# Second batch's attention heads as row-tiled pairs, with pair-wide values buffers and three rotating score buffers

## The chip, the cores and the metric

The kernel runs on one core of a Trainium2 chip. The time is the device time of one execution in microseconds, and the figure compared is the median of several runs. TensorE is called PE below, VectorE DVE, ScalarE ACT, GpSimd POOL, and SP is the engine whose queue issues nearly all DMA transfers of this kernel.

## The reference

Three stages follow one another: an attention over 4 batches of 8 heads (576 positions, head size 64), a gated MLP on its output, and a mixture of 8 experts with a route that is sticky along the sequence. Only the attention matters for the change:

```python
scores = scale * np.matmul(q, k.transpose(0, 1, 3, 2))
cum = np.cumsum(np.maximum(s, 0.0), axis=-1)
bias = -(cum[:, :, :, None] - cum[:, :, None, :])
scores = np.where(causal, -1000000000.0, scores + np.minimum(bias, 0.0))
attn = softmax(scores)          # maximum taken off, sum + 1e-09
out = np.matmul(attn, v)
```

## The kernel before, in words

**Precision.** float32 products are made of split operands: a value x is kept as a rounded part "hi" and the rest "lo", and a product takes hi·hi + hi·lo + lo·hi. The bias of a head is the cumulated sum `cum`, kept as 10 rows (5 query tiles, hi and lo) that a matmul with a 0/1 selection adds to the scores.

**Tiles.** A head has five query tiles `i`: four of 128 queries with 128·(i+1) keys, and a last one of 64 queries, which the two heads of a pair share as one 128-row tile (`emit_tail`, with block-diagonal queries `bdq` and selection `bdr` or `bds`). `prep_T` (L365) transposes q and k of a pair into a tile of four planes (q hi, k hi, q lo, k lo), head 0 of the pair on partitions 0 to 63, head 1 on 64 to 127.

**Two ways to the scores.** The first batch (pairs 0 to 3, `p < PR`) uses `emit_R` (L482): the two heads of a pair go through PE with 64 contraction rows each, one in the upper and one in the lower half of the array, four matmuls for each head and query tile (three of split products, one for the bias, from the constant `selc` and the bias rows `cumr`). The other three batches use `emit_S` (L501), one head at a time: `prep_asm` (L389) builds a stacked copy of the head by five DMAs (three from the pair's planes, 885 kB together: (3 + 1 + 2) planes of 64 x 576 floats; one of the head's 10 bias rows; the first time for each buffer also the selection rows `sel`), so that two matmuls of 128 and 74 contraction rows are enough for a query tile. `QK[0]` and `QK[1]` hold the stacked copies (in the first batch the pairs' planes), `QK[2]` the planes of the later pairs.

**Softmax and values.** `row_min` (L437, DVE) takes the scores out of PSUM with mask and row extreme, `soft` (L444) makes exp on ACT, adds 1e-9 on POOL, takes the reciprocal on DVE and scales on POOL. `emit_T` (L519) transposes the scaled tile on PE and copies it from PSUM into `et` by ACT or DVE. `emit_PV` (L544) multiplies by the values; heads 0 to 7 (`g < F4`) do it in plain float32. `emit_X` (L587) hands a pair's output on. In `emit_R` the first head's scaled tiles for i = 2, 3 lie in `E2`, `E3` (one buffer each), the second head's in tiles of the tag `ga` (two buffers for i = 2 and 3 together), which the MLP uses later.

**Order.** `R_steps` (L616) goes through the pairs of the first batch, five steps each; the list `AFTER` (L712) says how many steps later a pair's transposes (T), value products (P), value loads (V) and output (X) come, and what is over at the end (`left`) is worked off among the first steps of `A_steps` (L656), which handles the other heads with a lag of four tiles. `merge` interleaves a batch's attention with the MLP of the batch before (`M_steps`, L882; with `M0_steps`, L1443, for batch 0, which also prepares w_sg and w_out), by running sums of written costs; the MLP of batch 0 begins when the output of pair 3 is out. During the first batch the weights w_in are split (`W_steps`, L1418). A scheduler sets each engine's final order from this order by a simulated timeline. All loads and copies go through SP's queue in order (`dma`, L77). `prep_V` (L410) loads the values of one head into one of two buffers `vv`.

## Time and profile before

| what | value |
|---|---|
| median of 3 runs | 829.77 us (826.39 to 830.7) |
| the profiled execution's own time | 832.37 us |
| its span | 830.1 us |
| busy, share of span: PE | 785.8 us, 95% |
| PE weight loads | 675.5 us, 81% |
| DVE | 510.2 us, 61% |
| ACT | 436.0 us, 53% |
| POOL | 337.4 us, 41% |
| attention of batch 0 alone | from 10 us to about 80 us of the span |
| attention of batch 1 beside the MLP of batch 0 | about 80 us to 190 us |
| experts | from about 540 us |

The span is what the profile covers; the execution's own time adds what lies around it (2.3 us here). A busy PE means that at least one matmul is in the array by a modelled end, so it also counts the time in which a matmul only drains. The granted clock of PE is given as a share of full speed.

### The profile page before, as it was taken

The numbers are of one execution on the slowest core, as the hardware profiler recorded it, in microseconds if no ns is written. First come the engines' busy times: TensorE is split into PE (matmuls) and PEld (weight loads), VectorE is DVE, ScalarE is ACT, GpSimd is POOL, SyncE is SP. The second block draws the span as 40 slices with busy tenths as digits, with TensorE's granted clock in tenths as the row PEclk, the third lists the DMA queues.
The fourth block names the chain that finished last, engine by engine and source line by source line (L and its number), as shares of the span: only waits on it lengthen the run. The fifth ranks groups of instructions, "written<-read, shape, count | busy, mean of one in ns | idle before, by whom it ended". The sixth has DMA issues, their size and how long they took to land. (4 is left out here: it accounts for less than half of the span.)

```text
span 830.1 us, 14670 instructions
## 1 busy us (share of the span) xinstructions
PE 785.8 (95%) x4832; PEld 675.5 (81%) x4832; DVE 510.2 (61%) x1469; ACT 436.0 (53%) x1040; POOL 337.4 (41%) x614
## 2 busy tenths in 40 slices
PE   9887989899999999999999999989999999999995
PEld 5565877698789799789797778778988989899894
DVE  6787567685776789676884577664644445443420
ACT  6776567675547786246873254144544444444410
POOL 6787436575625578325684010060031220313101
PEclk9999999999999999989999999999999999999998
DMA  8568599845787575768442842153664444635401
GB/s 189 140 188 229 145 267 263 216 145 119 159 254 200 121 219 128 193 199 197 97 155 79 279 143 109 58 191 128 164 212 144 137 165 129 200 113 174 128 4 36
DMA packets 118041, 133.06 MB, mean 160 GB/s; under 512 B 69603, under 2 KB 83043, under 8 KB 117963
## 3 DMA queue, kind: packets, MB, share of 16 engines
q1 hardware_dynamic: 114123, 122.61, 53.6%
q0 software_dynamic: 3840, 9.48, 3.2%
q8 instruction: 40, 0.66, 0.3%
q14 instruction: 38, 0.31, 0.1%
HBM read 90.99 MB, written 22.95 MB: 137 GB/s over the span
## 5 line engine op out<-in xcount | busy, mean ns | idle before, releaser
L1241 DVE TENSOR_TENSOR wp<-wraw,wp 128x1024 fp32r<-128x1024 f32 x63 | 76.6, 1224 | 95.8 <-ACT wp L1240 91.3
L871 PE MATMUL ps<-wp,hT 128*128 128x512 f32 x528 | 123.0, 392 | 0.0
L871 PE MATMUL ps<-xT,wp 128*128 128x384 f32 x672 | 119.1, 336 | 0.0
L871 PEld LDWEIGHTS ps<-xT,wp 128*128 128x128 f32 x672 | 117.3, 188 | 0.7
L871 PEld LDWEIGHTS ps<-wp,hT 128*128 128x128 f32 x528 | 98.6, 188 | 21.1
L1297 POOL DMA_INDIRECT out_dram<-y,ids x24 | 29.4, 1224 | 212.3 <-ACT y L1296 175.0
L1240 ACT CAST wp<-wraw 128x1024 fp32r<-128x1024 f32 x64 | 66.5, 1049 | 62.6 <-DMA wraw<-in_moe_w_dram 56.0
L446 ACT ACTIVATE E<-E,negm 128x128 f32<-128x128 f32 (+4 forms) x136 | 79.4, 585 | 34.3 <-DVE negm L439 30.6
L450 POOL TENSOR_SCALAR E<-E,lsum 128x128 f32<-128x128 f32 (+4 forms) x136 | 77.8, 575 | 37.1 <-DVE lsum L448 28.3
L570 PE MATMUL ps<-et,vv 128*128 128x320 f32 (+9 forms) x476 | 82.5, 314 | 8.5 <-DVE et L537 5.2
L570 PEld LDWEIGHTS ps<-et,vv 128*128 128x128 f32 (+1 forms) x476 | 65.7, 173 | 22.8 <-DVE et L537 6.2
L439 DVE CUSTOM_DVE_ANT_0 E<-ps,zmask 128x128 f32<-128x128 f32 (+4 forms) x136 | 63.5, 471 | 17.9 <-PE ps L871 14.6
L447 POOL TENSOR_SCALAR lsum<-lsum 128x1 f32<-128x1 f32 (+1 forms) x128 | 31.2, 244 | 104.6 <-ACT E L446 88.3
L531 PE MATMUL ps<-ident,E 128*128 128x128 f32 (+1 forms) x452 | 67.6, 262 | 4.6 <-POOL E L450 1.6
L539 ACT CAST et<-ps 128x384 fp32r<-128x384 f32 (+3 forms) x120 | 50.2, 427 | 37.2 <-PE ps L531 35.3
L871 PE MATMUL ps<-wsg,vg 128*128 128x288 f32 x448 | 67.7, 302 | 0.8 <-DVE g L880 0.8
L871 PE MATMUL ps<-xh,w 128*128 128x288 f32 x256 | 59.3, 309 | 4.6 <-DVE wsg L857 2.9
L871 PEld LDWEIGHTS ps<-wsg,vg 128*128 128x128 f32 x448 | 62.0, 191 | 1.4 <-DVE g L880 1.0
L531 PEld LDWEIGHTS ps<-ident,E 128*128 128x128 f32 (+1 forms) x452 | 47.4, 140 | 16.5 <-issue 4.6
L540 DVE TENSOR_TENSOR et<-ps,et 128x384 fp32r<-128x384 f32 (+3 forms) x120 | 57.0, 481 | 4.6 <-ACT et L539 4.1
L871 PE MATMUL ps<-w,vg 128*128 128x512 f32 (+1 forms) x216 | 55.4, 400 | 0.0
L1285 DVE SCALAR_TENSOR_TENSOR hT<-ps,hT 128x384 fp32r<-128x384 f32 x56 | 30.3, 554 | 40.2 <-ACT hT L1284 40.0
(312 smaller groups left out, 1569.9 us busy)
## 6 DMA issues: line engine op xcount, KB each, us to landing
wraw<-in_moe_w_dram SPq DMA_DIRECT2D x64, 512.0 KB
qk<-qk SPq DMA_DIRECT2D x24, 432.0 KB
w<-wv_d SPq DMA_DIRECT2D x16, 512.0 KB
w<-wo_d SPq DMA_DIRECT2D x16, 512.0 KB
qk<-qk SPq DMA_DIRECT2D x24, 288.0 KB
w<-wu_d SPq DMA_DIRECT2D x12, 512.0 KB
nq<-in_q_dram SPq DMA_DIRECT2D x30, 144.0 KB
nk<-in_k_dram SPq DMA_DIRECT2D x30, 144.0 KB
```

The costliest lines, as they stand in the source:

```text
L439: hred[g] = DVE.tensor_tensor_reduce(out=e[:, a:z], in0=pt[:, 0:z - a], in1=zmask[:, m0:m0 + z - a], scale=-1.0, scalar=BIG if hi == 0 els ...
L446: ACT.activation(out=x, in_=x, func=ACTF.Exp, scale=-1.0, bias=nm, accum_out=l[:, z:z + 1])
L447: POOL.tensor_scalar(out=l, in0=l, scalar1=1e-9, scalar2=0.0, op0=ALU.add, op1=ALU.add)
L450: POOL.tensor_scalar(out=x, in0=x, scalar1=l[:, z:z + 1], scalar2=1.0, op0=ALU.mult, op1=ALU.mult)
L531: PE.transpose(pt[:, j * M:(j + 1) * M], e[h, 128 * j:128 * (j + 1)], ident[h, h])
L539: ACT.copy(out=dst[0], in_=src)
L540: DVE.tensor_tensor(out=dst[1], in0=src, in1=f32v(dst[0]), op=ALU.subtract)
L570: PE.matmul(x, lhsT=l, rhs=rhs if g >= F4 else f32v(rhs), start=(j == 0 and n_ == 0), stop=(j == js[-1] and n_ == len(ms) - 1),)
L871: ms = [PE.matmul(pt, lhsT=l, rhs=r, start=(first_ and x == 0), stop=(last_ and x == n - 1)) for x, (l, r) in enumerate(pairs)]
L1240: c = ACT.copy(out=w[:, 0, :], in_=r)
L1241: a = (POOL if (e, j) == (0, KD) else DVE).tensor_tensor(out=w[:, 1, :], in0=r, in1=f32v(w[:, 0, :]), op=ALU.subtract)
L1285: DVE.scalar_tensor_tensor(out=ht[:, 1, f, 0:w_], in0=pt[:, 0:w_], scalar=0.0, in1=f32v(ht[:, 0, f, 0:w_]), op0=ALU.max, op1=ALU.subtract)
```

## The change

It does five things. (1) `PR` becomes 8 pairs, so that `emit_R` also handles the second batch (heads 8 to 15); their bias rows come from `czp`, into which `batch_cum` loads 10 rows for each of 8 heads at pair 3, step 3; `tail_sel` rewrites `bds` for the shared tile of each pair. Stacked copies are made from head 16 on, the first one after the last step of pair 7. (2) Where `QK[2]` lay, a tile `QE` holds wide scaled tiles (i = 2, 3) until pair 8 needs the place: heads take `E2`/`E3`, planes 0 and 1 of `QE`, and planes 2 and 3 in turn by (g + 1) % 3, so that `ga` is used by head 15 alone. (3) In the first batch one `vv` tile holds the values of both heads of a pair, so that two buffers hold two pairs, and a pair's values are loaded two pairs ahead, at the step "V1" of `AFTER`. (4) In the second batch the loads are at "V0" and "V1", one pair ahead. (5) The selection rows of the stacked copies are saved to DRAM (`sel_d`) at the start and loaded from there.

```diff
@@ buffers
-    PR = PB
-    QK = [T(ap_, [128, 4, S], F32R, f"qk{i}") for i in range(3)]
+    PR = 2 * PB
+    QK = [T(ap_, [128, 4, S], F32R, f"qk{i}") for i in range(2)]
+    QE = T(ap_, [128, 4, S], F32, "qk2")
...
+    sel_d = dram.tile([2 * NQ, S], F32, name="sel_d")
@@ emit_sel
+        dma(sel_d, sel[64:KX])
@@ prep_T
         if c == 0:
+            if p == PR:
+                QK.append(T(ap_, [128, 4, S], F32R, "qk2"))
             Tst[p] = QK[p % 2 if p < PR else 2]
@@ prep_asm
-            dma(dst[64:KX, 2, :], sel[64:KX])
+            dma(dst[64:KX, 2, :], sel_d)
@@ new functions
+    def batch_cum():
+        for g in range(H, 2 * H):
+            z = 64 * (g % 2) + 16 * (g % H // 2)
+            dma(czp[z:z + 2 * NQ, :], cum_rows[g - H])
+
+    def tail_sel(p):
+        if p < PR:
+            for h in half:
+                POOL.tensor_copy(out=bds[h, h], in_=f32v(selc)[h, p % PB, NQ - 1:NQ].to_broadcast([64, 64]))
+        elif p == PR:
+            POOL.memset(f32v(bds), 0.0)
+            for r in range(2):
+                POOL.memset(f32v(bds)[64 * r:64 * r + 2, half[r]], 1.0)
@@ prep_V
+        if g < F4:
+            VV[g + 1] = vv
+            for r in range(2):
+                heads_in[g + r] = dma(f32v(vv[:, 0:NQ - 1, r, :]), v[b, h + r, 0:512, :].rearrange("(j p) d -> p j d", p=128)).ins.name
+            POOL.tensor_scalar(out=f32v(vv[:, NQ - 1]), in0=vt[:, h % VG:h % VG + 2, :], scalar1=1.0, scalar2=1.0, op0=ALU.mult, op1=ALU.mult)
+            return
...
-        if g < F4:
-            heads_in[g] = dma(f32v(vv[:, 0:NQ - 1, 0, :]), src).ins.name
-            POOL.tensor_scalar(out=f32v(vv[:, NQ - 1, 0, :]), in0=vt[:, h % VG, :], scalar1=1.0, scalar2=1.0, op0=ALU.mult, op1=ALU.mult)
-            return
@@ etile
-    def etile(i, r=0):
-        if r and i > 1:
-            return T(mp, [128, 512], F32, "ga", bufs=2)[:, 0:128 * i + 128]
+    def etile(i, g=None):
+        if g is not None and i > 1:
+            z = (g + 1) % 3
+            if g == 2 * PR - 1:
+                return T(mp, [128, 512], F32, "ga", bufs=2)[:, 0:128 * i + 128]
+            if z:
+                return QE[:, i - 2 if z == 1 else i, 0:128 * i + 128]
@@ tail_queries
+        if p >= PB:
+            tail_sel(p)
@@ emit_tail, emit_R
-        sel_, cz = (bdr[:, p], cumr) if p < PR else (bds, czp)
+        sel_, cz = (bdr[:, p], cumr) if p < PB else (bds, czp)
...
-        e = [etile(i, r) for r in range(2)]
+        e = [etile(i, 2 * p + r) for r in range(2)]
...
-                    l, m = selc[h, p, i:i + 1].to_broadcast([64, 128]), cumr[h, 0:n]
+                    l, m = selc[h, p % PB, i:i + 1].to_broadcast([64, 128]), (cumr if p < PB else czp)[h, 0:n]
@@ emit_PV
-                ms = [(f32v(vv[0:kk, j, 0, :]), 0)]
+                ms = [(f32v(vv[0:kk, j, r, :]), 0)]
@@ A_pro
         prep_V(0)
-        prep_V(1)
+        prep_V(2)
@@ R_steps
-            if p == PR - 1 and i == 0:
-                prep_T(PR, 0)
-                prep_T(PR, 1)
-                prep_load(PR + 1)
-            if i == 0:
-                for x in when:
-                    if 2 * p <= when[x] < 2 * p + 2:
-                        prep_asm(x)
+            if (p, i) == (PB - 1, 3):
+                batch_cum()
...
+            if p == PR - 1 and i > 2:
+                prep_T(PR, i - 3)
+                if i == 4:
+                    prep_load(PR + 1)
+                    for x in when:
+                        if when[x] < 2 * PR:
+                            prep_asm(x)
@@ after
-        elif g + 2 < NH:
-            prep_V(g + 2)
+        elif x[1] == "1" or p >= PB:
+            n = 2 * p + 2 + int(x[1])
+            if p < PB:
+                n = 2 * p + 4 if p + 2 < PB else 2 * PB + p + 2 - PB
+            prep_V(n)
```

## Rows read from the trace of the kernel before

**Rows 1.** Windows view, three stretches: busy by engine (instructions), granted PE clock, DMA share, GB/s.

```profile
40.00:60.00 20.00, 17.46 (x124) 12.39 (x124) 17.11 (x47) 15.09 (x42) 16.98 (x24) 1.00 0.65 182
100.00:120.00 20.00, 17.06 (x137) 15.85 (x136) 12.56 (x40) 12.80 (x42) 5.27 (x14) 1.00 1.01 254
300.00:320.00 20.00, 20.00 (x159) 19.51 (x157) 16.94 (x55) 13.83 (x39) 15.66 (x30) 1.00 0.85 224
```

**Rows 2.** PE's waits, span 0 to 80 us: waiter, releaser, total us, times, longest.

```profile
PE ps L570 <- DVE et L537: 5.2, 4, 1.6
```

**Rows 3.** Windows view around two stalls, columns as in rows 1.

```profile
80.00:84.00 4.00, 1.92 (x15) 1.35 (x14) 1.52 (x6) 1.48 (x5) 2.07 (x5) 1.00 0.86 222
84.00:88.00 4.00, 4.00 (x15) 2.21 (x13) 0.00 (x0) 0.76 (x2) 0.34 (x1) 0.57 0.02 4
...
160.00:164.00 4.00, 4.00 (x20) 2.81 (x19) 0.26 (x4) 3.07 (x8) 3.76 (x10) 0.63 0.92 192
```

**Rows 4.** PE's waits, 80 to 160 us, columns as in rows 2.

```profile
PE ps L871 <- DVE wsg L857: 2.9, 1, 2.9
PE ps L570 <- DMA vv<-in_v_dram: 2.1, 1, 2.1
PE ps L531 <- DVE lsum L448: 1.4, 2, 1.2
PE ps L871 <- DVE negm L439: 1.2, 2, 1.0
```

**Rows 5.** PE's timeline, row-tiled steps of pair 2: start, length, line.

```profile
41.27 0.55 PE L496 MATMUL ps<-qk 64*128 64x128 f32 x6
...
41.87 0.98 PE L531 MATMUL ps<-ident,E 128*128 128x128 f32 x7
...
45.59 0.80 PE L496 MATMUL ps<-qk 64*128 64x384 f32 x6
...
46.49 0.47 PE L375 MATMUL ps<-ident,nq 96*128 96x96 f32 x3
...
50.25 0.97 PE L496 MATMUL ps<-qk 64*128 64x512 f32 x6
...
51.29 0.94 PE L531 MATMUL ps<-ident,E 64*128 64x64 f32 x8
```

**Rows 6.** PE's timeline, stacked heads: start, length, line.

```profile
103.38 0.52 PE L871 MATMUL ps<-qk 128*128 128x384 f32 x2
103.74 0.60 PE L531 MATMUL ps<-ident,E 128*128 128x128 f32 x4
104.09 0.72 PE L871 MATMUL ps<-qk 128*128 128x512 f32 x2
104.65 0.60 PE L850 MATMUL ps<-ident,vg 128*128 128x128 f32 x4
...
106.85 0.41 PE L871 MATMUL ps<-qk 128*128 128x128 f32 x2
107.10 0.40 PE L531 MATMUL ps<-ident,E 128*128 128x128 f32 x2
```

**Rows 7.** DVE's timeline, pair 3, tile i = 2 of both heads.

```profile
66.85 0.53 DVE L439 CUSTOM_DVE_ANT_0 E<-ps,zmask 128x384 f32<-128x384 f32 x1
...
69.69 0.56 DVE L439 CUSTOM_DVE_ANT_0 ga<-ps,zmask 128x384 f32<-128x384 f32 x1 [0.92 <-PE ps L531]
```

**Rows 8.** SP's queue, 76 to 80 us: start, length, transfer.

```profile
76.11 3.42 SPq L78 DMA_DIRECT2D qk<-qk  x2
79.65 0.54 SPq L78 DMA_DIRECT2D vv<-in_v_dram  x1
```

**Rows 9.** SP's queue at 112 us, a load of w_out.

```profile
112.24 1.82 SPq L78 DMA_DIRECT2D vg<-in_moe_w_out_dram  x1
```

**Rows 10.** DVE's timeline where that load is awaited.

```profile
119.19 0.43 DVE L754 TENSOR_SCALAR vg<-vg 128x512 int32<-128x512 int32 x1 [4.95 <-DMA vg<-in_moe_w_out_dram]
```

**Rows 11.** Lines view by form: POOL's copies into the shared tile's queries.

```profile
L468 POOL CAST bdq<-qk 64x128 fp32r<-64x128 f32 x32 | 9.9, 310 | 8.0 <-DVE qk L382 6.1 <-PE ps L871 0.7
```

More of the change, by code (lines that the diff above doesn't have):

```diff
@@ L190 @@
     vt = T(ap_, [128, 4, D], F32, "vt")
+    KX = 64 + 2 * NQ
+    sel_d = dram.tile([2 * NQ, S], F32, name="sel_d")
     cum_d = dram.tile([2, NQ * (NH - H), S], F32, name="cum_d")
@@ L269, in emit_cum @@
         dma(cum_d.rearrange("z p s -> p z s"), ch)
-    KX = 64 + 2 * NQ
     cum_rows = cum_d.rearrange("z (i g) s -> g (z i) s", g=NH - H)
@@ L323 @@
         POOL.memset(f32v(x), 0.0)
-    for r in range(2):
-        POOL.memset(f32v(bds)[64 * r:64 * r + 2, half[r]], 1.0)
     POOL.memset(vt, 0.0)
@@ L411, in prep_V @@
         b, h = divmod(g, H)
-        r = S - 512
         if g % VG == 0:
-            dma(vt[0:r], v[b, h:h + VG, 512:S, :].rearrange("h p d -> p h d"))
+            dma(vt[0:S - 512], v[b, h:h + VG, 512:S, :].rearrange("h p d -> p h d"))
         vv = T(ap_, [128, NQ, 2, D], F32R, "vv", bufs=2)
         VV[g] = vv
+        if g < F4:
[4 more added lines that the diff above has]
+            return
         src = v[b, h, 0:512, :].rearrange("(j p) d -> p j d", p=128)
-        if g < F4:
-            heads_in[g] = dma(f32v(vv[:, 0:NQ - 1, 0, :]), src).ins.name
-            POOL.tensor_scalar(out=f32v(vv[:, NQ - 1, 0, :]), in0=vt[:, h % VG, :], scalar1=1.0, scalar2=1.0, op0=ALU.mult, op1=ALU.mult)
-            return
         vr = T(ap_, [128, NQ - 1, D], F32, "vr", bufs=2)
```

## The prediction

> **What bounds the kernel now.** I read the windows view first. In the last attention batches PE is in use all the time: 20.00 of 20 us at 300 to 320 us [rows 1]. From there to the end nothing in the diff acts, so a microsecond saved or lost earlier goes into the time one for one. Before that PE is not full: 17.46 of 20 us in the first batch, 17.06 at 100 to 120 us, where the DMA share stands at 1.01 [rows 1]. So the change can only win by closing holes of PE in the first 190 us. The waits view names them. In the first batch the value products wait for a copy by DVE, 5.2 us in four waits [rows 2]. After it one wait of 2.1 us is for the load of values, one of 2.9 us is put down to a DVE instruction, and 1.4 and 1.2 us are for the softmax chain [rows 4]. A hole costs more than its length: after the first of them the granted clock was 0.57 for 4 us with PE busy throughout, and 0.63 in another such stretch [rows 3]. A row at 0.57 loses 4 x 0.43 = 1.7 us, at 0.63 1.5 us.
>
> **Scores of batch 2 as pairs (what it adds).** Start to next start, a row-tiled step of two heads took 0.60, 0.90 and 1.04 us with 128, 384 and 512 keys [rows 5]. A stacked head took 0.25, 0.36 and 0.56 us [rows 6], two heads 0.50, 0.72 and 1.12. The differences are +0.10, +0.18 and -0.08 us; for 256 keys, where I show no row, I take the middle of its neighbours, +0.14. That is +0.34 us a pair, **+1.4 us** for four pairs. If all 16 steps went like the best they would give -1.3 us, like the worst +2.9. So the pairs themselves save PE nothing; matmuls are halved in width of the array but doubled in number. The steps of rows 5 already stand between full-array work, so entering and leaving the tiled form is in them.
>
> The Trainium skill, "TensorEngine Tiling (Array Packing)", section "Tiling Modes", says that a change of tiling mode drains TensorE, which speaks against putting 16 tiled steps between the full-array matmuls of the MLP. It gives no price. Were the whole excess of rows 5 over the bare columns such a drain (2.54 us against 4 x 1024 columns at 2.4 GHz = 1.71, so 0.28 a step) and new in each step, 16 steps would cost 4.4 us in place of 1.4. The trace speaks for the smaller figure, since the stacked steps have 0.63 us of such excess over the same three tiles without any mode change.
>
> **Stacked copies that fall away.** Eight heads' copies, 885 kB each by their shapes, go: 7.1 MB of DMA, with four to five issues for each head on SP and two for each pair's `czp`; 8 loads of `batch_cum` and one of `sel_d` come in. This bears on two holes. At 76 us two copies held SP's queue for 3.42 us, and the values load issued only at 79.65 [rows 8], for which PE then waited 2.1 us [rows 4]. And a load of w_out issued at 112.24 [rows 9] came only at 119.19, after DVE had stood still for 4.95 us [rows 10], all engines of the transfer at 1.01 [rows 1]; behind DVE stood the PE wait of 2.9 us. In that window 254 GB/s x 20 us = 5.1 MB moved, of which two heads' copies are 1.8 MB, a third. The rest, the weights being loaded and stored, stays. I take half of the hole, **-1.5 us**, between 0 and -2.9.
>
> **Values for a pair, two pairs ahead.** The load of rows 8 is replaced by one that is issued a whole pair earlier, so the 2.1 us hole goes, and the low clock behind it (1.7 us). But the MLP of batch 0 begins when pair 3 is out, and five steps of pair 4 now run before that, in the manner of the first batch. Such a pair takes about 20 us and leaves PE empty for 20 - 17.46 = 2.5 us [rows 1]; with the gain of the next part, 1.2. So 2.1 + 1.7 - 1.2 = **-2.6 us**, between 0 (another wait in the same place) and -3.8. In batch 2 the values come one pair ahead, two steps before use; a step there is some 5 us (110 us for 20), so the load is covered.
>
> **Wide tiles in an idle buffer.** In pair 3 DVE took the first head's 384-key tile at 66.85 and the second's at 69.69, after 0.92 us of standing still until a PE transpose gave a `ga` buffer free [rows 7]. That transpose stood in PE's queue behind the value product that waited for DVE. Three rotating places undo this circle. But the product still waits for the copy of the shared tile, which DVE does after the row extremes. So half of the 5.2 us [rows 2]: **-2.5 us**, between 0 and -5.2.
>
> **Smaller edits.** `tail_sel` adds two 64 x 64 copies on POOL per pair; the nearest row is 310 ns for a 64 x 128 copy [rows 11], so 8 x 0.31 = 2.5 us in all, hidden by POOL's 5.27 of 20 us [rows 1]; bare, they would stand on the way to the shared tile, one tile in each pair. They wait for the last pair's shared tile to leave PE, as the copies into `bdq` beside them already do. `soft` is called half as often, which frees POOL and DVE a little: 0. The first stacked copy (head 16) moves from five steps ahead of its use to none: its transposes, five transfers and their landing come between pair 7's last step and head 16. By rows 8 three such copies hold SP 5 us, and with landing some 8 us pass. What hides them is what pair 7 still has open and the MLP of batch 0, which goes on beyond the end of the second batch; bare it would cost those 8 us. I take 0.
>
> **The sum.** +1.4 - 1.5 - 2.6 - 2.5 = -5.2 us. Against the profiled execution (832.4 us) that is 827.2. That one stands 2.6 us above the median of the runs, 829.8, so for the median I say **824.6 us**. All bounds together give -1.3 - 2.9 - 3.8 - 5.2 = -13.2 (816.6), or with no gain +2.9 (832.7).
>
> **The rivals.** *Bursts on DVE (slower).* A pair sends two row extremes, two exps and two scalings into the in-order queues at once, and the MLP's chains stand behind them. For: with one head at a time PE already waited 1.4 + 1.2 us for this chain between 80 and 160 us [rows 4], and one such wait was followed by 1.5 us of lost clock [rows 3], together 4.1 us. Against: DVE is at 12.6 of 20 us at 100 to 120 [rows 1] and its work falls slightly. If these waits triple, +8.2 us; DVE would then also be what holds the first batch and the load of w_out, so only the values part stays: 829.8 + 1.4 - 2.6 + 8.2 = 836.8 us. With those gains void it is slower by more than 0.5% from 4.2 + 1.2 = 5.4 us of new waits on.
>
> *The holes were not the copies' and not `ga`'s.* The first batch's waits are DVE's order, and w_out is late from the weight traffic, so only +1.4 - 2.6 = -1.2 remains: 828.6 us. For: the releaser is a DVE copy, not a buffer [rows 2]. Against: the second head's row extreme did wait for one [rows 7].
>
> *All of it.* Every hole closes: some 817 us. For: of the 12.8 us that stand in rows 2 and 4, 10.2 hang on buffers or transfers that change [rows 2, 4]. Against: closing a hole shows the next one.
>
> *The change does not do what it says:* the scheduler might set other matmuls between the halves of a pair, so that they no longer run side by side. Fully apart, a step with 512 keys takes 8 x 0.28 (half of the stacked head's 0.56) = 2.2 us in place of 1.04 [rows 5, 6]; four pairs at that ratio give about +15 us (1.15 x 3.29 us x 4). I count it among the slower cases with a small share, since both halves are ready at once.
>
> **How the numbers follow.** Forecast 0.41 (its own range 820 to 829), not the copies' 0.23, all of it 0.14, bursts 0.20, halves apart 0.02. Half a percent, 4.1 us, is about what a measurement of this kernel can tell from no change. Faster by more (below 825.6): 0.28 of the forecast, all of 0.14, 0.05 of the second, 0.47. Slower by more (above 833.9): 0.17 of the bursts, 0.02, and 0.01 of the second, 0.20. The rest, 0.33, is the same. The range is 814 to 836: down past the sum of the bounds by part of the 4.1 us of the softmax waits, up to where the bursts stand.
>
> **What would show it.** In the profile after: no PE wait for values near 80 us and no clock of 0.57 behind it; no DVE wait on PE before a second head's row extreme; PE's wait for DVE's copy in the first batch halved; DMA share below 1 at 100 to 120 us and DVE's wait for w_out shorter; tiled steps in batch 2 at 0.6 to 1.04 us. I am wrong if PE's waits for row extremes or reciprocals between 80 and 190 us grow by more than 5 us, if PE stands before head 16 waiting for its stacked copy, or if the waits of rows 2 stay at 5 us.

## The result: 0.75% slower, and the profile after

The median of five runs went from 829.77 to **835.33 us** (832.94 to 836.12), ratio 1.0075 with an interval of 1.0053 to 1.0097. The forecast was 824.6 us and faster; the kernel is slower by more than the half percent that a measurement can tell.

The first lines to read are those that answer to the rows of the prediction. PE's windows after (columns as in [rows 1]), with four more stretches:

```profile
28.00:32.00 4.00, 2.44 (x20) 1.65 (x18) 1.59 (x7) 2.27 (x7) 0.46 (x2) 1.00 1.01 213
32.00:36.00 4.00, 3.24 (x9) 1.63 (x10) 3.42 (x11) 1.75 (x5) 0.93 (x2) 0.68 1.01 276
40.00:60.00 20.00, 17.85 (x123) 12.32 (x122) 17.20 (x54) 14.80 (x42) 15.99 (x24) 1.00 0.51 147
80.00:84.00 4.00, 3.86 (x28) 2.42 (x26) 0.86 (x5) 2.63 (x7) 3.54 (x8) 1.00 0.31 83
84.00:88.00 4.00, 4.00 (x40) 3.11 (x40) 2.74 (x12) 3.09 (x12) 2.97 (x6) 1.00 0.72 189
100.00:120.00 20.00, 20.00 (x167) 18.25 (x166) 15.29 (x44) 15.88 (x49) 8.03 (x16) 1.00 0.50 133
```

PE's waits of the kernel after, first 0 to 80 us, then 80 to 160 us (columns as in [rows 2]):

```profile
PE ps L596 <- DVE et L563: 5.1, 4, 2.3
PE ps L557 <- POOL E L470: 3.6, 2, 1.8
...
PE ps L625 <- ACT xf L608: 2.3, 2, 1.6
PE ps L901 <- DVE negm L459: 0.2, 1, 0.2
```

DVE's timeline of the kernel after: the loads that it waited for at the start, and the load of w_out.

```profile
27.45 0.18 DVE L834 CAST wgl<-gl 128x36 fp32r<-128x36 f32 x1 [1.78 <-DMA gl<-in_moe_w_local_dram]
...
31.85 0.46 DVE L1458 TENSOR_SCALAR bbc<-bbc 128x576 f32<-128x576 f32 x1 [2.17 <-DMA bbc<-in_moe_b_sg_dram]
...
114.98 0.43 DVE L784 TENSOR_SCALAR vg<-vg 128x512 int32<-128x512 int32 x1 [0.52 <-DMA vg<-in_moe_w_out_dram]
```

Beside [rows 1] and [rows 4] one sees that the holes after 80 us closed, and more fully than forecast. PE is busy 20.00 of 20 us at 100 to 120 us where it was 17.06, the DMA share there is 0.50 for 1.01, the waits for the values, for w_sg, for the softmax sums are gone, and so is the clock of 0.57 at 84 to 88 us [rows 3]. DVE's longest wait for w_out is 0.52 us for 4.95 [rows 10]. In the first batch nothing was won: 5.1 us of waiting for DVE's copy, as before [rows 2]. And there is a new hole at 26 to 34 us with the clock down behind it.

So the waits went, and the kernel became slower all the same. The outputs of pairs 0, 3, 4 and 8 show where. PE's timeline of the kernel before has as first lines of them (start, length):

```profile
38.68 0.44 PE L599 MATMUL ps<-ident,xf 128*128 128x128 f32 x2
93.34 0.91 PE L599 MATMUL ps<-ident,xf 128*128 128x128 f32 x3
132.16 0.71 PE L599 MATMUL ps<-ident,xf 128*128 128x128 f32 x5
257.11 0.60 PE L599 MATMUL ps<-ident,xf 128*128 128x128 f32 x4
```

PE's timeline of the kernel after has, for the same four outputs:

```profile
43.30 0.90 PE L625 MATMUL ps<-ident,xf 128*128 128x128 f32 x3
97.53 0.44 PE L625 MATMUL ps<-ident,xf 128*128 128x128 f32 x2
130.76 0.38 PE L625 MATMUL ps<-ident,xf 128*128 128x128 f32 x2
260.60 0.60 PE L625 MATMUL ps<-ident,xf 128*128 128x128 f32 x4
```

4.6 us were lost before the first output, the first batch then kept its pace, 5.6 us were regained between pairs 3 and 4, and 4.9 us were lost again from there to pair 8, where the kernel was 3.5 us behind.

**A ledger for PE.** To separate work from waits and clock I took PE's timeline from its first instruction to the start of its last row (the 16.6 us of that row, alike in all kernels, are left out), split it into idle time (as the timeline shows it) and the rest, and multiplied the rest by the granted clock, window by window of 1 us. The product is called PE time at full clock; what the multiplication takes off is the clock's loss.

| us | before | after | difference |
|---|---|---|---|
| PE time at full clock | 760.5 | 770.5 | +10.0 |
| idle | 32.4 | 28.2 | -4.2 |
| lost to the clock | 10.0 | 5.0 | -5.0 |
| up to the output of pair 8 alone: time, idle, clock | 231.3, 19.7, 5.1 | 243.0, 15.0, 1.7 | +11.6, -4.7, -3.4 |

In these two profiles waits and clock give 9.2 us back, but PE has 10 us more to do. The clock's part belongs to these two executions alone: in the other profiles below its loss runs from 6.2 to 22.7 us, whatever the second batch. The profiled executions themselves stand only 0.6 us apart (832.37 and 832.94), since the one of before lay above all five of its runs (826.4 to 830.7) and the one of after was the fastest of its five. Span times mean granted clock takes the clock out: 815.9 to 817.1 us in the mean of 79 runs of before on four chips, 821.7 +- 0.4 in the five of after, 4.9 us more. That is near +10.0 - 4.2.

The measure is not exact. It runs low where much of the work fell on the low clock: from the output of pair 8 to that of pair 15 it gave 179.9 us in e3_early and f3_vals below, with nothing lost to the clock there, and 178.6 in the kernel before, with 3.1 us lost. Over like kernels it repeats within some 2 us.

### The profile page after: what moved, and what is told of

It is laid out like the page before. It is cut to its first block, busy times and chain, and to the rows that moved or that the text cites. A ratio compares the mean times of both kernels' runs of the same rounds, so it can differ in the third digit from the quotient of the medians.

```text
span 831.1 us, 14646 instructions
## 1 busy us (share of the span) xinstructions
PE 790.8 (95%) x4896; PEld 674.1 (81%) x4896; DVE 511.5 (62%) x1453; ACT 436.8 (53%) x1040; POOL 338.9 (41%) x603
## 5 line engine op out<-in xcount | busy, mean ns | idle before, releaser
L1327 POOL DMA_INDIRECT out_dram<-y,ids x24 | 33.5, 1397 | 209.0 <-ACT y L1326 165.1
L596 PE MATMUL ps<-et,vv 128*128 128x320 f32 (+8 forms) x476 | 80.9, 309 | 7.2 <-DVE et L563 5.1
L466 ACT ACTIVATE E<-E,negm 128x128 f32<-128x128 f32 (+4 forms) x122 | 69.8, 573 | 27.2 <-DVE negm L459 24.5
L470 POOL TENSOR_SCALAR E<-E,lsum 128x128 f32<-128x128 f32 (+4 forms) x122 | 71.4, 589 | 30.6 <-DVE lsum L468 22.3
L565 ACT CAST et<-ps 128x384 fp32r<-128x384 f32 (+4 forms) x120 | 49.4, 426 | 34.3 <-PE ps L557 31.0
L467 POOL TENSOR_SCALAR lsum<-lsum 128x1 f32<-128x1 f32 (+1 forms) x112 | 27.0, 242 | 97.5 <-ACT E L466 85.9
L459 DVE CUSTOM_DVE_ANT_0 E<-ps,zmask 128x128 f32<-128x128 f32 (+4 forms) x122 | 54.4, 454 | 15.6 <-PE ps L901 8.9
L566 DVE TENSOR_TENSOR et<-ps,et 128x384 fp32r<-128x384 f32 (+4 forms) x120 | 56.9, 483 | 10.9 <-ACT et L565 10.6
L557 PE MATMUL ps<-ident,E 128*128 128x128 f32 (+1 forms) x403 | 58.2, 260 | 5.4 <-POOL E L470 3.9
L557 PEld LDWEIGHTS ps<-ident,E 128*128 128x128 f32 (+1 forms) x403 | 41.5, 140 | 15.9 <-POOL E L470 4.4
```

Of the source, the lines that this page charges most:

```text
L459: hred[g] = DVE.tensor_tensor_reduce(out=e[:, a:z], in0=pt[:, 0:z - a], in1=zmask[:, m0:m0 + z - a], scale=-1.0, scalar=BIG if hi == 0 els ...
L466: ACT.activation(out=x, in_=x, func=ACTF.Exp, scale=-1.0, bias=nm, accum_out=l[:, z:z + 1])
L470: POOL.tensor_scalar(out=x, in0=x, scalar1=l[:, z:z + 1], scalar2=1.0, op0=ALU.mult, op1=ALU.mult)
L557: PE.transpose(pt[:, j * M:(j + 1) * M], e[h, 128 * j:128 * (j + 1)], ident[h, h])
L565: ACT.copy(out=dst[0], in_=src)
L566: DVE.tensor_tensor(out=dst[1], in0=src, in1=f32v(dst[0]), op=ALU.subtract)
```

## The experiments

Every kernel ran beside runs of the kernel before on the same chip; there were four chips. PE time, idle and clock's loss are read from one profile each, as above; the first output is that of pair 0.

| run | ratio to before | PE time | idle | clock | first output |
|---|---|---|---|---|---|
| before | 1 | 760.5 | 32.4 | 10.0 | 38.7 |
| after | 1.0075 [1.0053, 1.0097] | 770.5 | 28.2 | 5.0 | 43.3 |
| e1_late | 1.0063 [1.0031, 1.0096] | 768.3 | 29.9 | 13.0 | 42.6 |
| e3_early (of before) | 1.0040 [1.0005, 1.0076] | 759.7 | 32.1 | 6.5 | 39.0 |
| f3_vals (of before) | 1.0047 [1.0016, 1.0078] | 761.0 | 29.1 | 8.4 | 41.9 |
| f1_vlater | 1.0061 [1.0036, 1.0086] | 769.1 | 25.6 | 11.9 | 44.8 |
| h2_again | one run, 835.26 us | 769.3 | 26.6 | 10.0 | 40.5 |
| e4_ga | 1.0067 [1.0035, 1.0098] | 770.2 | 27.0 | 8.0 | 42.8 |
| f4_novals | 1.0099 [1.0063, 1.0134] | 769.5 | 24.8 | 11.9 | 44.9 |
| f2_copy | 1.0119 [1.0091, 1.0146] | 769.5 | 28.4 | 11.2 | 43.1 |
| e2_paired | 1.0052 [1.0019, 1.0084] | 768.7 | 30.4 | 10.1 | 42.6 |
| g1_rows (of before) | 1.0193 [1.0092, 1.0293] | 771.3 | 31.1 | 8.4 | 40.0 |
| g2_full (of before) | 1.0114 [1.0016, 1.0212] | 764.6 | 34.7 | 22.7 | 47.7 |
| g3_six | 1.0228 [1.0162, 1.0294] | 762.5 | 35.9 | 17.3 | 43.0 |
| g4_two | 1.0069 [1.0028, 1.0111] | 767.9 | 27.2 | 9.7 | 41.0 |
| h3_fix | 1.0060 [1.0036, 1.0083] | 767.3 | 28.4 | 6.2 | 42.2 |

The profile of g2_full is of a run with a lower clock than its others (mean 0.969), so of that run only PE's own rows and its time at full clock are used. One column carries the study. The kernel before and the two variants of it that keep its work have 759.7 to 761.0 us of PE time; every kernel whose whole second batch is row-tiled has 767.3 to 770.5. In the mean of the seven of these that are not chained (see below) it is 769.5, some 9 us more than the 760.4 of the first three.

The ratios hold the clock too: in the mean of its runs every variant was granted less of it (0.971 to 0.986) than the kernel before (0.987 to 0.989). e3_early and f3_vals are 0.4 to 0.5% slower by that alone: their span times clock is that of before. Why, no run shows.

### The start

Two things of the change could have delayed the first pair: four stores of the split w_in (`wu_d`), which slipped forward to 27 us, and the two loads of the second pair's values. SP's queue of the kernel after shows both (start, length, transfer):

```profile
11.58 2.28 SPq L78 DMA_DIRECT2D vv<-in_v_dram  x4
...
16.15 4.13 SPq L78 DMA_DIRECT2D u<-in_s_dram  x5
...
26.78 0.50 SPq L78 DMA_DIRECT2D bbc<-in_moe_b_sg_dram  x1
27.38 0.38 SPq L78 DMA_DIRECT2D wu_d<-w  x1
```

**e1_late** holds the stores back in the kernel after, **e3_early** pulls them forward in the kernel before:

```diff
@@ e1_late, M0_steps of after
-            if ustore and n >= UN:
+            if ustore and n >= UN and H + 2 in heads_in:
...
@@ e3_early, stores of before
-                        'last', wu_d[:, :, z,
+                        9 if kt < 2 else 'last', wu_d[:, :, z,
...
```

> The changed kernel with one edit: the stores of the split w_in halves (wu_d) wait, as before the change, until the values load of head 10 has been written. Theory (the stores' place): in the changed kernel four of these stores slipped to 27 to 34 us, because the load they are ordered behind became that of head 9; they hold the DMA engines while DVE and ACT wait for other loads, and the output of pair 0 came at 43.3 us, 4.6 us later than before. Then here the first pair's output is back near 38.7 us and the time is 4 to 6 us below the changed kernel, about 830 us. Rival (wide tiles and values loads themselves slow the start): no store before 80 us, but the first pair's output stays near 43 us and the time within 1.5 us of the changed kernel, 835.

> The kernel before with one edit: the first four stores of the split w_in halves are ordered behind the values load of head 9, as they came to be in the changed kernel; nothing else changes. Theory (the stores' place): they slip to about 25 to 35 us and the output of pair 0 comes 3 to 5 us later than 38.7 us; the time rises by 3 to 5 us, to 833 to 835. Rival (the stores are harmless, or taking them out of the crowded stretch at 100 to 120 us pays for it): within 1.5 us of 829.8.

Without the stores the first output stayed at 42.6 us; with them, in the kernel before, it stayed at 39.0, and span times clock was 816.2 +- 0.8 us against 816.8 +- 0.3 beside it. The theory of the stores falls.

**f3_vals** puts the pair-wide values of the first batch alone into the kernel before:

```diff
@@ prep_V, first batch
-            heads_in[g] = dma(f32v(vv[:, 0:NQ - 1, 0, :]), src).ins.name
+            VV[g + 1] = vv
+            for r in range(2):
+                heads_in[g + r] = dma(f32v(vv[:, 0:NQ - 1, r, :]), v[b, h + r, 0:512, :].rearrange("(j p) d -> p j d", p=128)).ins.name
...
@@ A_pro
         prep_V(0)
-        prep_V(1)
+        prep_V(2)
...
```

> The kernel before, with the pair-wide values of the first batch alone (two loads and one tile for a pair, two pairs ahead); the second batch goes one head at a time as before. Theory: this part alone moves the first output from 38.7 to 42 to 43.5 us (+4), and it alone also brings the gain at the start of the second batch, so that the wait for values near 82 us and the low clock behind it are gone and the step from the output of pair 3 to that of pair 4 falls from 38.9 us to 35 or less; both together leave the time within 0.3% of before. Rival: the start is late from something that comes with the row-tiled second batch (the order of the constants, the store of the selection rows); then the first output here is at 39 us and this part alone gains 3 to 4 us (ratio 0.995 to 0.996).

The first output came at 41.9 us. DVE's timeline of this run shows the wait of the kernel after, and its windows (columns as in [rows 1]) the hole of PE and the clock behind it:

```profile
30.68 0.46 DVE L1430 TENSOR_SCALAR bbc<-bbc 128x576 f32<-128x576 f32 x1 [2.55 <-DMA bbc<-in_moe_b_sg_dram]
```

```profile
26.00:28.00 2.00, 0.92 (x7) 0.71 (x8) 1.96 (x7) 0.55 (x3) 1.72 (x4) 1.00 0.89 150
28.00:34.00 6.00, 5.75 (x22) 3.46 (x21) 2.94 (x9) 3.37 (x11) 1.15 (x3) 0.50 0.50 147
```

After a hole of about 1 us PE ran 6 us at half its clock, 1.2 GHz. Without the 3.3 us that the clock took up to there, the first output would stand at 38.6 us, where it was before; so this run shows DVE's wait, but the lateness in it is the clock's. The step from pair 3 to 4 fell from 38.8 to 36.9 us, less than the fall to 35 expected. But the wait for values and the low clock behind it lie ahead of pair 3's output in the kernel before [rows 3], and from the output of pair 0 to that of pair 4 this run took 88.0 us for 93.5: the values alone bring nearly the whole gain of the kernel after (87.5). Gain and loss cancel: span times clock is 817.1 +- 0.6 us, that of before on the same chip 817.1 +- 0.3.

**f1_vlater** keeps the changed kernel and moves the two loads behind that of b_sg; **h2_again** is the same kernel once more.

```diff
@@ prep_V (x is the load)
...
+                if g == 2:
+                    behind(x, hred[max(hred)].ins.name)
@@ A_pro
-        prep_V(2)
@@ R_steps
+            if (p, i) == (1, 1):
+                prep_V(2)
```

> The changed kernel, with the second pair's values (two loads) put behind the other loads of the start, behind the load of b_sg (bbc), instead of directly behind the first pair's. Theory: these two loads, in SP's in-order queue ahead of the loads of w_in, s, w_gate and b_sg, are what made the first pair late (its output began at 43.3 us in place of 38.7). Then gl and bbc no longer hold DVE (1.8 and 2.2 us after the change), the first output comes at 39 to 40.5 us, the later pairs of the first batch too are 3 to 4 us earlier, and the median falls by 2 to 4 us against the changed kernel's ratio of 1.0075, to some 1.003. Rival: something else of the start (the store of the selection rows, the place of the values tiles' POOL copies) made it late; then the first output stays at 42.5 or later and the ratio at 1.006 to 1.008.

> The changed kernel with the second pair's values behind the other loads of the start, once more, for its start alone: in the first profile of it the waits of DVE for gl and bbc were gone, but PE had the clock at half from 9 to 20 us and the first output came at 44.8 us. Theory (the place of these loads made the first pair late): with the clock at full there, the first output comes at 39 to 40.5 us. Rival: it stays at 42 us or later at full clock.

In f1_vlater DVE no longer waited for gl and bbc, but the first output came at 44.8 us: PE had stood still for 1.2 us at 6 us, before the first products for the bias, and had half its clock from 9 to 20 us. So this run's first output says nothing on the loads as it stands. In h2_again the clock was full there, and the output came at 40.49, DVE's wait for bbc at 0.8 us. Its windows show 0.58 at 28 to 32 us, so another 1.7 us (4 x 0.42) are the clock's:

```profile
8.00:26.00 18.00, 17.29 (x118) 10.44 (x117) 13.45 (x47) 13.70 (x41) 11.72 (x29) 1.00 0.82 189
26.00:28.00 2.00, 0.81 (x8) 0.59 (x8) 1.91 (x10) 1.19 (x4) 1.45 (x3) 0.99 0.91 220
28.00:32.00 4.00, 4.00 (x20) 2.79 (x19) 2.88 (x10) 1.46 (x5) 1.54 (x5) 0.58 0.99 290
```

One run does not settle it: h3_fix below, with the same start, had no long wait of DVE for bbc either, yet came at 42.2 us, with half the clock for 6.8 us from 25 us on. All profiles together do better. With the clock's loss up to there taken off, the first output stands at 38.0 to 39.4 us in the seven profiles without the early loads (h3_fix at 39.4; g2_full left out), at 39.7 to 42.6 in the seven of changed kernels with them, and at 38.6 in f3_vals. So in the changed kernel the place of the second pair's values in SP's queue costs some 2 to 3 us, and the rest of the 4.6 is the clock's, 1.7 us in the profile after. The ratio hardly moved (1.0061), so the start is not the main part of the loss.

### The wide tiles, the values, the first stacked copy

**e4_ga** gives the first batch its old tiles back (second heads in `ga`); **f4_novals** undoes the values part of the change; **f2_copy** makes the first stacked copy three steps earlier.

```diff
@@ e4_ga, etile
+            if g < H:
+                z = 0
-            if g == 2 * PR - 1:
+            if g == 2 * PR - 1 or g < H and g % 2:
@@ f4_novals, A_pro (prep_V, emit_PV and after as in the kernel before)
-        prep_V(2)
+        prep_V(1)
@@ f2_copy, etile and R_steps
+            if g >= 2 * PR - 4:
+                z = 0
-            if g == 2 * PR - 1:
+            if g >= 2 * PR - 4 and g % 2 == 0:
-            if p == PR - 1 and i > 2:
-                prep_T(PR, i - 3)
-                if i == 4:
+            if p == PR - 1 and i < 2:
+                prep_T(PR, i)
+                if i == 1:
```

> The changed kernel with the first batch's wide tiles of the second heads in the two ga buffers as before the change (first heads in E2 and E3); the second batch keeps the three rotating places. The prediction's theory (the buffer circle costs half of 5.2 us): slower than the changed kernel by 2 to 3 us, about 838. Rival (DVE's order sets the pace of the first batch: outputs of pairs 0 to 3 are 18.1, 19.9 and 16.3 us apart after, 18.2, 20.0 and 16.4 before): within 1 us of the changed kernel.

The first batch kept its pace (42.8, 61.3, 81.3, 97.6 us for its four outputs, after: 43.3, 61.4, 81.3, 97.5), so three rotating places gained nothing over one and two.

> The changed kernel without the pair-wide values: one head's values in a tile, loaded one pair ahead, as before; the second batch in row-tiled pairs and the wide tiles in QE stay. Theory: the first output is back at 38.7 to 39.5 us; the wait for values near 82 us stays away or comes back with some 2 us, as the load no longer stands behind stacked copies; what remains is the row-tiled batch itself, so the loss between the outputs of pairs 7 and 8 is all there (44 us) and the ratio is 1.000 to 1.004. Rival: the row-tiled second batch by itself costs nothing on the path, and the whole of the loss is the start's: then the ratio is 0.994 to 0.999. If the start stays at 42 us or later, the values loads were not its cause.

Even without the values part the kernel is at 1.0099, and the rival (0.994 to 0.999) is out. Most of that ratio is the clock's, though: span times clock is 819.7 +- 1.0 us against 817.1 +- 0.3, 2.6 us of the 8. The wait for values near 82 us did not come back, and DVE's longest wait for w_out was 0.5 us, where f3_vals, with the stacked copies, still had 3.5. From the output of pair 0 to that of pair 4 it took 87.4 us. So the values part and the row-tiled batch each bring this gain by themselves, and it is not had twice. Its first output at 44.9 us has the same cause as in f1_vlater, half the clock from 9 to 20 us, so the expectation for the start could not be read.

> The changed kernel, with the planes of pair 8 and the stacked copy of head 16 made three steps earlier, at steps 0 and 1 of pair 7 instead of 3 and 4; for that the wide tiles of heads 12 to 15 lie in E2/E3 and in ga, so that the place of QE is free earlier. Theory: the late first stacked copy is what was lost between the output of pair 7 and that of pair 8 (44.4 us in place of 38.0); then that distance falls to 40 us or less, PE's empty time between 200 and 220 us (2.75 us) falls below 1 us, and the ratio falls from 1.0075 to about 1.002. Rival: the distance is made by the order of the MLP of batch 0 against the attention, or by what else is left open at the end of the second batch; then the distance stays within 2 us of 44 and the ratio does not change, or the ga tiles shared with the MLP cost something on top (up to 3 us).

PE was busy 19.98 of 20 us at 200 to 220 us (17.25 after), as expected. But the distance from pair 7 to pair 8 stayed at 43.4 us and the kernel got slower, 1.0119: the idle time only moved ahead (28.4 us in all, as after). That distance is no loss by itself; in the kernel after, more of the MLP of batch 0 is still open when pair 7 is out.

### What PE does longer

Three of the 16 row-tiled steps of the second batch had other matmuls between the two heads. One of them in PE's timeline of the kernel after, and below it one that stayed whole:

```profile
144.59 0.79 PE L522 MATMUL ps<-qk 64*128 64x384 f32 x3
145.21 0.34 PE L522 MATMUL ps<-czp,selc 64*128 64x384 f32 x1
145.48 0.49 PE L901 MATMUL ps<-w,xl 128*128 128x512 f32 x1
145.90 0.79 PE L522 MATMUL ps<-qk 64*128 64x384 f32 x3
146.53 0.34 PE L522 MATMUL ps<-czp,selc 64*128 64x384 f32 x1
...
121.35 0.97 PE L522 MATMUL ps<-qk 64*128 64x512 f32 x6
122.15 0.41 PE L522 MATMUL ps<-czp,selc 64*128 64x512 f32 x2
122.40 0.46 PE L557 MATMUL ps<-ident,E 64*128 64x64 f32 x5
```

The whole step takes 1.05 us to the next start, as in [rows 5]. The split one takes 0.89 + 0.90 = 1.79 in place of 0.90. The three together cost 2.7 us. **e2_paired** chains the eight matmuls of a step:

```diff
-                PE.matmul(pt[r][:, 0:n], lhsT=l, rhs=m, start=(x == 0), stop=(x == 3))
+                y = PE.matmul(pt[r][:, 0:n], lhsT=l, rhs=m, start=(x == 0), stop=(x == 3))
+                if prev:
+                    behind(y, prev[0])
+                prev[:] = [y.ins.name]
...
```

> The changed kernel with the eight matmuls of each row-tiled step bound in their order, so that no other matmul stands between the two heads. Theory (halves apart): in the changed kernel 3 of the 16 steps of the second batch ran one head after the other (1.33, 1.79 and 2.24 us in place of 0.69, 0.90 and 1.04), 2.7 us of PE in a stretch where PE is full, so the time falls by 2 to 3 us, to about 832.5. Rival (binding only moves the wait: a step then waits for its second PSUM buffer): the steps run at 0.6 to 1.04 us but PE waits as much elsewhere; within 1 us of the changed kernel.

PE time fell by 1.8 us (and by 2.0 from h2_again to h3_fix, which differ by the chain alone); the ratio is 1.0052. Profiles of like kernels differ by as much, but the row-tiled score matmuls by themselves say the same: those of both batches took 29.4 to 30.5 us at full clock, start to next start, in the seven unchained kernels and 26.9 to 27.8 in the three chained ones. The term is real, and a fifth of the 10 us.

**g1_rows** and **g2_full** price the way into the row-tiled form by itself, in the kernel before:

```diff
@@ emit_S
+        if H <= g < 2 * H:
+            ys = []
+            for h in half:
+                ys.append(PE.matmul(ps()[:, 0:128], lhsT=qk[h, 0, qs], rhs=qk[h, 1, 0:128], start=True, stop=True))
+            behind(ys[1], ys[0].ins.name)
@@ g2_full: the same but for
-            for h in half:
+            for h in (slice(0, 128), slice(0, 128)):
```

> The kernel before, with two spare matmuls added behind the scores of every stacked query tile of the second batch (32 tiles): each with 64 contraction rows and 128 keys, one in the upper and one in the lower half of the array, into score buffers that nobody reads. Work is added, nothing is left out. PE's busy time times its granted clock, summed over the span, is called PE time at full clock here; it was 760.5 us in the kernel before, 759.7 and 761.0 in its two variants, and 768.3 to 770.5 in the seven profiles with a row-tiled second batch: some 9 us more, where the prediction had 1.4. Theory: a good part of that is paid at each entry into and exit from the row-tiled form, by the neighbours too, 0.25 to 0.3 us a time; then these 32 pairs cost 8 to 10 us of PE time at full clock more than the same pairs in the full array, though they stream half the columns. Rival: entry and exit cost nothing; then they cost the same as the full-array pairs or up to 3 us less, and the 9 us lie elsewhere (scores that stream more columns, transposes that come in bunches).

> The same 64 spare matmuls in the kernel before, each with 128 contraction rows and 128 keys, so in the full array like everything around them. A stacked tile of 128 keys took 0.25 us with two such matmuls, so 32 pairs should add some 8 us of PE time at full clock (less what hides under neighbouring weight loads, at least 4): 764 to 769. It is the yardstick for the run with the row-tiled pairs: theory says that one has 8 to 10 us more, the rival 0 to 3 us less.

The lines view by form, the spare matmuls of g1_rows, then of g2_full (count, busy us, mean ns):

```profile
L510 PE MATMUL ps<-qk 64*128 64x128 f32 x64 | 11.4, 324 | 0.3 <-DVE et L545 0.2
```

```profile
L510 PE MATMUL ps<-qk 128*128 128x128 f32 x64 | 11.8, 261 | 0.1
```

PE time was 771.3 us with the row-tiled pairs and 764.6 with the full-array ones: 6.7 us more for 32 pairs, 0.21 us each, though the two of a row-tiled pair can run side by side. Of this 5.4 us, 0.17 each, can be found at the pairs: 1.7 in the spare matmuls' own starts (9.56 us to the next start against 7.83), 3.0 on the matmul directly ahead (0.26 us to the next start in the mean against 0.17) and 0.7 on the one behind. One such place in PE's timeline, g1_rows and then g2_full:

```profile
111.97 0.42 PE L876 MATMUL ps<-qk 128*128 128x128 f32 x2
112.32 0.33 PE L510 MATMUL ps<-qk 64*128 64x128 f32 x2
112.58 0.44 PE L536 MATMUL ps<-ident,E 128*128 128x128 f32 x2
...
118.41 0.42 PE L876 MATMUL ps<-qk 128*128 128x128 f32 x2
118.66 0.39 PE L510 MATMUL ps<-qk 128*128 128x128 f32 x2
118.89 0.41 PE L536 MATMUL ps<-ident,E 128*128 128x128 f32 x2
```

The stacked scores ahead take 0.35 us to the next start in place of 0.25. The other 1.3 us stand elsewhere and may be the measure's, since the profile of g2_full lost far more to the clock. So the price is **0.17 to 0.21 us** a time, under the 0.25 to 0.3 expected, and the rival, that entry and exit are free, is out. The mean spans differ the same way (span times clock 825.6 +- 0.9 against 821.9 +- 0.5).

**g4_two** issues the steps of 128 and 256 keys of a pair as one chained stretch, 12 entries for 16; **g3_six** row-tiles six pairs in place of eight.

```diff
@@ g4_two, R_steps (with the chain of e2_paired)
-            emit_R(p, i) if i < NQ - 1 else emit_tail(p)
+            if i == NQ - 1:
+                emit_tail(p)
+            elif p < PB:
+                emit_R(p, i)
+            elif i != 1:
+                emit_R(p, i)
+                if i == 0:
+                    emit_R(p, 1)
...
@@ g3_six (etile: z = (g + 2) % 3)
-    PR = 2 * PB
+    PR = 6
```

> The changed kernel with each row-tiled step chained together and, in the second batch, the steps of 128 and 256 keys of a pair issued as one stretch, so that there are 12 entries into the row-tiled form in place of 16. The chained kernel alone had 768.7 us of PE time at full clock. Theory: four entries fewer save 1.0 to 1.2 us of it: 767.5, ratio 1.003 to 1.005. Rival: nothing is paid at an entry: 768.5 or more. Both heads' row extremes then come four at a time, so PE's waits for score buffers may grow by a microsecond or two in either case.

767.9 us against 768.7 in e2_paired: in the theory's direction, but profiles of like kernels differ by as much, so it decides nothing.

> The changed kernel with six row-tiled pairs in place of eight (the first batch and half of the second); heads 12 to 15 go stacked again, and the wide tiles rotate so that the last row-tiled head has ga. Theory: the row-tiled form costs the second batch 2.3 us of PE time at full clock for each pair, so half the dose is found: 764.5 to 766 us, and the time is between the two kernels (ratio 1.002 to 1.006). Rival: the extra comes once, from how the second batch ends or from the wide tiles, not by the pair; then it is all there (768 or more) or all gone (762 or less).

Neither was met. PE time was 762.5 us, a fifth of the extra for half the dose. But with 17.3 us lost to the clock the measure runs low here, so this run does not tell whether the price goes by the pair. The time was the worst of all, for another reason: where the form changes inside a batch, PE stood before the first stacked head, which the prediction had named as a risk for head 16. PE's timeline of this run, and the windows there:

```profile
137.31 0.61 PE L901 MATMUL ps<-qk 128*128 128x128 f32 x2 [4.05 <-DMA qk<-qk]
```

```profile
130.00:150.00 20.00, 13.64 (x73) 10.88 (x72) 5.17 (x15) 5.68 (x16) 6.75 (x12) 0.77 1.02 266
```

13.64 of 20 us busy, at a clock of 0.77, with the DMA share at 1.02.

**h3_fix** joins the two repairs, the chain and the later values.

> The changed kernel with both repairs that the runs so far point to: the second pair's values behind the other loads of the start, and the matmuls of each row-tiled step chained, so that nothing stands between its halves. Theory: PE time at full clock 767 to 769 us (as in the chained kernel; before 760.5), the empty time of PE some 3 us less than in the changed kernel, ratio 1.001 to 1.004: better than the changed kernel, still not faster than before, as the entries into the row-tiled form and the longer transposes stay. Rival: the 9 us of PE time are no loss, since what holds the kernel is waits; then the two repairs bring it to 0.997 or below.

PE time was in the range given (767.3), but idle time did not fall (28.4) and the ratio stayed at 1.0060. No version found here beats the kernel before.

## Why the prediction was wrong

**The step that failed** is the first term of the sum: that the pairs "save PE nothing" and cost +1.4 us, because "entering and leaving the tiled form is in" the steps of [rows 5]. PE time at full clock rose by 10.0 us in the two profiles, by some 9 in the mean of like kernels. By rows, start to next start: the scores took 2.1 us more (15.7 for the 128 new row-tiled matmuls, 13.6 less for stacked ones), the transposes of scaled tiles 3.3, the products with the gate weights (128 x 18) 1.2, the scores of the shared tiles 1.0, all others 2.2. Of the 15.7 us 2.7 are the three steps torn apart, of which the chain gave 1.8 to 2.0 back. Without them the scores would have cost 0.6 us less than before, where +1.4 was forecast. So the start-to-start sum is not what failed. What failed is the premise that these starts hold the whole price: nothing was put down for the other rows of PE, which took 7.7 us more.

The measure was the mistake. Start to next start of the tiled matmuls leaves out what the instruction ahead of them pays, and g1_rows against g2_full shows that most of the price stands there. For 16 steps 0.17 to 0.21 us make 2.7 to 3.4 us. The transposes show it in both kernels: one that stands directly ahead of a row-tiled score takes 0.20 us to the next start (8 such before, 18 after), ahead of another transpose 0.12, ahead of a stacked score 0.05 (42 before, 25 after). At these lengths the changed places come to some 2.3 of the 3.3 us. The 8 in the kernel before could have been read in its first batch ahead of the prediction. For the rest, 1.0 us on transposes and 4.4 on gate products, shared tiles and other rows, no run tells what part the entries have. So about half of the 10 us stays open.

By the rule of the page "TensorEngine Tiling (Array Packing)", section "Tiling Modes", of the Trainium skill, a change of tiling mode drains TensorE. g1_rows and g2_full agree that the change has a price, at 0.17 to 0.21 us, where the 0.28 us a step beside that rule in the prediction was an estimate; that the price is a drain no run shows. I had set the rule aside on the argument that the stacked steps show 0.63 us of excess too, which compares two things of which neither was the entry.

**Stacked copies (-1.5) and values (-2.6): right that they close the waits.** From the output of pair 0 to that of pair 4 PE's idle time fell by 7.2 us (12.7 to 5.5) and the clock's loss by 1.7, while PE had 2.9 us more to do, so the kernel after gained 6.0 us there. The softmax waits are in this too. The copies' part is seen in DVE's wait for w_out, 4.95 us before, 3.5 in f3_vals, 0.5 in f4_novals. The wait for values is gone in both of these, in f4_novals even without the pair-wide loads; there the stacked copies no longer stand ahead of the load in SP's queue. So the two terms were not independent, as the sum took them.

**Wide tiles (-2.5): wrong.** The waits of [rows 2] stayed at 5.1 us, one of the signs named for being wrong, and e4_ga ran at the same pace. The rival that put these waits down to DVE's order was right that the buffers are not the cause; that DVE's order is, no run shows.

**What was not in the sum at all** is the start. I costed the values two pairs ahead only where they are used; the loads had also to be issued somewhere, and they went ahead of several others in SP's queue. Price: some 3 us late for most of those in the kernel after, and some 2 to 3 of the 4.6 us at the first output.

**Rivals.** The bursts on DVE did not come: the waits for row extremes and reciprocals shrank to 0.2 us. *Halves apart*, given 0.02, came for 3 of 16 steps; I had worked it out only as all or nothing. No case had the row-tiled form itself as what makes it slower, beyond a bound of +2.9.

**The smaller edits at 0** held: `tail_sel` took 8 x 235 ns = 1.9 us on POOL, and PE did not stand before head 16 for its copy, though it stood 4.05 us before the first stacked head of g3_six.

## What to carry to other kernels

A kernel with PE almost full is priced by PE's own work first; waits that close beside it are worth their length, and in this kernel a form that puts PE through more changes of tiling paid at each change, mostly on the neighbours' rows. Count PE time at the granted clock before and after: it came out within some 2 us in like kernels whose spans did not (768.3 us in a span of 838.6, 770.5 in one of 831.1). And a load that is moved earlier has a place in a queue: name what it now stands in front of.

## What was not expected of the hardware

A hole of PE of about 1 us was followed by 3 to 10 us at half the clock in some profiles, and whether a hole had that effect differed between runs of like kernels: in the kernel before PE was idle 0.97 of 2 us at 26 us and kept its clock, in f3_vals 1.08 of 2 us there and lost it for 6 us. In f1_vlater and f4_novals a stop of 1.2 and 1.3 us at 6 us was followed by half the clock from 9 to 20 us; f3_vals stopped there for 1.2 us too and kept it. The clock's loss in the profiles ran from 5.0 to 22.7 us, a spread wider than any edit here was worth.
